# A spectral filter with a gated feed-forward block: the first product over two groups of 256 tokens, its weight tile loaded sooner and scaled alone, with four smaller edits

## The chip, the cores and the metric

The kernel runs on one core of a Trainium2 chip. The metric is device time in microseconds (us) of one execution. Before the change the median of three executions is 1207.04 us (1206.02 to 1208.09).

## The reference

One input `x` of 2048 tokens by 1024 features is normalised per token. The normalised rows `xn` go two ways: through a two-dimensional real FFT, a product with a complex filter and the inverse FFT (`s`), and through a feed-forward block with SiLU and 3584 hidden features. The output is the input plus the product of the two.

```
def _A_ref(x, w_r, w_i):
    X = rfft2(x, axes=(-2, -1))
    X = X * (w_r + 1j * w_i)
    return irfft2(X, (S, D), axes=(-2, -1))

def _B_ref(x, w1, w2):
    h = silu(einsum("bsd,df->bsf", x, w1))
    return einsum("bsf,fd->bsd", h, w2)

xn = layernorm(x)
s = _A_ref(xn, A_w_r, A_w_i)
g = silu(_B_ref(xn, B_w1, B_w2))
out = x + s * g
```

## The kernel before

Everything that TensorE multiplies is split into a high and a low float16 half, so each product is three matmuls: high by high, high by low, low by high. The tokens come in four chunks `c` of 512, each of four pieces `p` of 128 (a token of piece `p` of a chunk is every fourth row). The hidden features come in 28 tiles `f` of 128. The work has three long stages, and the spectral work is fed into the gaps between their matmuls.

**The first product** (`mm1`, matmuls on L500, PSUM tile `pa`) runs over pairs (c, f): 24 matmuls of 512 columns each, 8 slices of the 1024 features times 3 terms. The first six pairs are chunk 0 with f = 0 to 3, then chunk 1 with f = 0 and on. `evac` turns `pa` into hidden values with ScalarE. **The second product** (`mm2`, L584 to L586, PSUM tile `pb`) runs seven products `m` of eight blocks `j`, with weights `w2t` and hidden tiles `ht` read back from DRAM; `ht` has seven buffers, so a load of `ht` is issued when TensorE has done with an older one. The forward FFT along the features (`fa`), the filter stage (`fx`, L1070) and the inverse (`iu` on L1350 and L1358, `id` on L1439) are cut into small steps that a planner hands out between the matmuls.

The order of the instructions on every engine is fixed when the program is built, and each engine runs its own list in that order. Steps of the generators stand in lists: `bg` (layer norm, then the FFT stages) and `wq` (weights). At the start the order is written by hand in three tables: `FIRST` (the steps of the layer norm of chunk 0: `s` statistics, `n` normalise, `t` transpose on TensorE, `h` the high half, `l` the low half), `ENTRY` (what is done inside the first five products: `b` a step of `bg`, `w` a step of `wq`, `f` a group of 24 `fa` matmuls, `e` its evacuation) and `WARM` (idle matmuls on the constant `ones`, called `spin`, between steps).

What the change touches at the start:

- `weights1`: loads a raw tile `w1r` of w1, takes its largest absolute value with VectorE (`m`, L312), sums over partitions with a small TensorE matmul into the PSUM tile `s` (L293), makes a power of two from it (`e`, `r`, `rs` on L319 to L322, `s1` on GpSimd), then the high half `w` with ScalarE (L284) and the low half with VectorE (L287). Tiles 0 and 1 are scaled as a pair, 2 and 3 as a pair, 4 and 5 alone.
- `ln_gen`: statistics with VectorE (L780 to L783), the scale `v` with three small GpSimd operations (L785 to L787), the normalisation with ScalarE (L788). For chunk 0 TensorE transposes the pieces (PSUM tiles `tp`, L803 and L805); `hi` (L809) and `lo` (L816 with L817, or L819) write both halves of `xnT`. Pieces 0 to 2 transpose into the two large PSUM buffers `ft`, piece 3 into two small ones `ff`. Chunk 1 goes through `entering`: normalise into `xp` (L788), round to `xs` (L758), subtract for the low half (L766, VectorE), then four DMA transposes. On ScalarE's list the second pair of weight tiles (w_2, w_3) stands behind the normalisation of the first two pieces of chunk 1.
- The main body issues the loads on SP's queue: `x` pieces 0 to 3 and the identity, then `w1r` 0 to 2, then the constants.

What it touches later: `low_z` stores the filtered planes `zq` into `zd` (L1101 for even c, L1104 for odd c), `load_i` reads them back into `zt` with the constants `kk` (L1308 to L1312), `edge_in` copies one column into `zt` (L1319), `i_gen.mat` multiplies `zt` by `kk` (PSUM `iu`), `mat2` multiplies by the constants `ci` (PSUM `id`), and `edge_gen` has nine small float32 matmuls (`eps`, L1231 to L1233).

Of the kernel before, what the change touches and what calls it, by code (L numbers as in the profile page):

```python
# [25 lines left out]
WARM = [35, 8, 0, 0, 0, 12, 0, 0, 0, 0]  # L26
# [7 lines left out]
FIRST = ('s0 n0 s1 n1 t0 h0 s2 t1 h1 n2 s3 n3 l0', 't2 h2 t3 h3', 'l1 l2 l3')  # L34
ENTRY = ("fbwb||ew", "bbbwbb|bwwbb|f", "fwwbbw|wbbb|wb", "|wew|wf", "w||w")
# [118 lines left out]
def spectral_ffn(ctx, tc, x, w_r, w_i, w1, w2, ca, kc, ci, tw, pm, out):  # L154
    nc = tc.nc
# [21 lines left out]
    zd = [dp.tile([128, 2, 4, 2, 512] if c % 2 else [128, 4, 2, 1024], F16, name=f"zd{c}") for c in range(4)]  # L177
# [118 lines left out]
    def weights1():  # L296
# [43 lines left out]
        for i in range(3):  # L340
            load(i)
# [149 lines left out]
    def mm1(c, f, between={}):  # L491
        ps = J.pop("first", None) or pf.tile([128, 512], F32, name=f"pa{c}_{f}", tag="ff")
# [252 lines left out]
    def entering(c, stats, norm):  # L745
# [28 lines left out]
    def ln_gen(c):  # L774
# [17 lines left out]
        def trans(p):  # L792
            if p < 3:
                ps = pt.tile([128, 8, 128], F32, name=f"tp{c}_{p}", tag="ft")
                pst[p] = [(slice(0, 8), ps)]
            else:
                pst[p] = [(slice(d, d + 4), pf.tile([128, 4, 128], F32, name=f"tp{c}_{p}_{d}", tag="ff")) for d in (0, 4)]
            xt = A["x"].pop((c, p))
            xv = xt.rearrange("s (d0 d1) -> s d1 d0", d1=8)
            for ds, ps in pst[p]:  # L800
                for d in range(ds.start, ds.stop):
                    if p in (2, 3):
                        nc.tensor.matmul(ps[:, d - ds.start], xv[:, d], A["ident"], start=(d % 4 == 0), stop=(d % 4 == 3), is_transpose=True, skip_group_check=True)  # L803
                    else:
                        nc.tensor.transpose(ps[:, d - ds.start], xv[:, d], A["ident"])  # L805

        def hi(p):
            for ds, ps in pst[p]:
                nc.scalar.activation(xnT[c][:, 0, ds, p * 128:(p + 1) * 128], ps, AF.Copy)  # L809

        def lo(p):
            sl = slice(p * 128, (p + 1) * 128)
            for ds, ps in pst.pop(p):
                if p in (2, 3):
                    for d in range(0, ds.stop - ds.start, 4):
                        nc.tensor.matmul(ps[:, d:d + 4], A["minus"], xnT[c][:, 0, ds.start + d:ds.start + d + 4, sl], start=False, stop=True, skip_group_check=True)  # L816
                    nc.scalar.activation(xnT[c][:, 1, ds, sl], ps, AF.Copy)  # L817
                    continue
                nc.vector.tensor_tensor(xnT[c][:, 1, ds, sl], ps, xnT[c][:, 0, ds, sl], op=OP.subtract)  # L819
# [209 lines left out]
    def f_gen():  # L1029
# [174 lines left out]
    def edge_gen():  # L1204
# [96 lines left out]
    def load_i(c):  # L1301
        zt = C["p"].tile([128, 8192], F16, name=f"zt{c}", tag="zt", bufs=1)
        if c % 2:
            src = zd[c].rearrange("(m e) r q h x -> r m e (q h) x", e=2)
            dst = zt.rearrange("m (e k x) -> m e k x", e=2, k=8)
            for r in range(2):
                for e in range(2):
                    nc.sync.dma_start(dst[64 * r:64 * r + 64, e], src[r, :, e])  # L1308
# [259 lines left out]
    with tc.manual_schedule():  # L1568
# [73 lines left out]
        for k, q in enumerate((bg, wq, wq, bg, wq, wq, bg, wq, wq)):  # L1642
# [3 lines left out]
            if k == 4:  # L1646
                J["first"] = pf.tile([128, 512], F32, name="pa0_0", tag="ff")
# [150 lines left out]
```

## Time and profile before

| what | value |
|---|---|
| median of three executions | 1207.04 us |
| the profiled execution's own time | 1207.29 us |
| its span, first to last instruction | 1205.5 us |
| TensorE busy | 1195.1 us (99%) |
| VectorE busy | 1009.7 us (84%) |
| ScalarE busy | 511.6 us (42%) |
| GpSimd busy | 210.2 us (17%) |
| granted TensorE clock, mean | 0.999 of full speed |

Times are microseconds from the first instruction. PE is TensorE, DVE is VectorE, ACT is ScalarE, POOL is GpSimd, SP is the engine that issues nearly all DMAs. Matmuls are pipelined: each is shown some 0.16 us longer than the distance to the next one (a 512-column matmul is shown as 0.38 us and the next starts 0.216 us later), so work on TensorE is counted from start to start.

### The profile page before, as it was taken

The numbers are of one execution on the slowest core, as the hardware profiler recorded it, in microseconds if no ns is written. First come the engines' busy times: TensorE is split into PE (matmuls) and PEld (weight loads), VectorE is DVE, ScalarE is ACT, GpSimd is POOL, SyncE is SP. The second block draws the span as 40 slices with busy tenths as digits, with TensorE's granted clock in tenths as the row PEclk, the third lists the DMA queues.
The fourth block names the chain that finished last, engine by engine and source line by source line (L and its number), as shares of the span: only waits on it lengthen the run. The fifth ranks groups of instructions, "written<-read, shape, count | busy, mean of one in ns | idle before, by whom it ended". The sixth has DMA issues, their size and how long they took to land.

```text
span 1205.5 us, 18361 instructions
## 1 busy us (share of the span) xinstructions
PE 1195.1 (99%) x6600; PEld 597.1 (50%) x6600; DVE 1009.7 (84%) x1971; ACT 511.6 (42%) x698; POOL 210.2 (17%) x297
## 2 busy tenths in 40 slices
PE   8999999999999999999999999999999999999998
PEld 5544445444544544444444444445455545555555
DVE  7778986996799598669968999999279898998696
ACT  7775654366466463445524233132032222343212
POOL 2330041102402300411100111125031231100000
PEclk9999999999999999999999999999999999999999
DMA  8788698589989976889989999993997989989577
GB/s 263 182 192 213 199 268 242 173 248 281 294 251 278 275 227 197 195 197 205 183 234 246 284 239 261 237 305 131 261 333 219 367 308 329 363 319 343 175 242 267
DMA packets 279540, 302.24 MB, mean 251 GB/s; under 512 B 47956, under 2 KB 206932, under 8 KB 278548
## 3 DMA queue, kind: packets, MB, share of 16 engines
q1 hardware_dynamic: 275848, 291.69, 81.1%
q0 software_dynamic: 3312, 9.24, 4.5%
q8 instruction: 52, 0.85, 0.3%
q14 instruction: 40, 0.33, 0.1%
q10 hardware_dynamic: 288, 0.13, 0.0%
HBM read 183.94 MB, written 110.77 MB: 244 GB/s over the span
## 4 chain that ended last, share of the span: by engine, by line
PE 93%; DVE 3%; DMA 3%; issue 1%; SPq 1%; ACT 0%; POOL 0%; ACTq 0%; DVEq 0%
PE pa L500 48%; PE pb L584 12%; PE pb L585 12%; PE pb L586 12%; PE id L1439 2%; PE fx L1070 2%; DMA ht<-hd 2%; PE iu L1358 1%; PE iu L1350 1%; PE fa L837 1%; PE fa L838 1%; PE fa L839 1%; DMA w<-in_B_w_dram 0%; DVE Z L1192 0%; SPq L1104 0%
## 5 line engine op out<-in xcount | busy, mean ns | idle before, releaser
L500 PE MATMUL pa<-xnT,w 128*128 128x512 f16 x2688 | 584.0, 379 | 0.0
L500 PEld LDWEIGHTS <-w 128*128 128x128 f16 x2688 | 261.6, 98 | 311.9 <-issue 0.3
L584 PE MATMUL pb<-w,ht 128*128 128x512 f16 (+2 forms) x812 | 300.4, 372 | 1.0 <-DMA ht<-hd 1.0
L585 PE MATMUL pb<-w,ht 128*128 128x512 f16 (+2 forms) x812 | 300.4, 372 | 0.0
L586 PE MATMUL pb<-w,ht 128*128 128x512 f16 (+2 forms) x812 | 300.3, 372 | 0.0
L509 ACT ACTIVATE h<-pa,s 128x512 f32<-128x512 f32 x112 | 75.9, 681 | 153.4 <-PE pa L500 112.8
L586 PEld LDWEIGHTS <-ht 128*128 128x128 f16 x812 | 79.5, 98 | 91.0
L584 PEld LDWEIGHTS <-ht 128*128 128x128 f16 x812 | 79.5, 98 | 87.7 <-DMA ht<-hd 1.1
L585 PEld LDWEIGHTS <-ht 128*128 128x128 f16 x812 | 79.5, 98 | 86.5
L284 ACT ACTIVATE w<-jr,sc 128x512 f16<-128x512 f32 x98 | 67.5, 712 | 64.6 <-POOL jr L457 60.4
L287 DVE SCALAR_TENSOR_TENSOR hoone<-h,hs,hoone 128x2048 f16<-128x2048 f32 x28 | 65.6, 2342 | 17.0 <-ACT hoone L284 17.0
L287 DVE SCALAR_TENSOR_TENSOR w<-jr,sc,w 128x512 f16<-128x512 f32 x98 | 78.0, 803 | 0.0
L1192 POOL TENSOR_TENSOR Z<-yb 128x32 f32<-128x32 f32 x64 | 34.9, 573 | 224.9 <-DVE yb L1169 224.9
L284 ACT ACTIVATE hoone<-h,hs 128x2048 f16<-128x2048 f32 x28 | 55.9, 1997 | 18.4 <-DMA hd<-hoone 18.4
L457 POOL TENSOR_TENSOR jr<-jr,w 128x512 f32<-128x512 f32 x28 | 38.8, 1387 | 123.8 <-DMA w<-in_B_w_dram 75.9
L1092 ACT ACTIVATE zq<-Z,zs 128x1024 f16<-128x1024 f32 x16 | 18.4, 1148 | 91.5 <-DVE Z L1192 54.3
L287 DVE SCALAR_TENSOR_TENSOR hosum<-hr,hs,hosum 128x1536 f16<-128x1536 f32 x28 | 50.7, 1811 | 7.2 <-ACT hosum L284 7.2
L284 ACT ACTIVATE hosum<-hr,hs 128x1536 f16<-128x1536 f32 x28 | 43.9, 1569 | 20.5 <-DMA hd<-hosum 12.1
L539 DVE TENSOR_TENSOR hr<-h 128x1024 f32<-128x1024 f32 x28 | 34.1, 1218 | 18.3 <-ACT h L509 18.0
L678 ACT ACTIVATE pl<-pl,c 128x512 f32<-128x512 f32 (+2 forms) x28 | 17.4, 655 | 72.7 <-DVE pl L654 42.4
L284 ACT ACTIVATE w<-w1r,rs 128x1024 f16<-128x1024 f32 x28 | 32.0, 1143 | 27.8 <-DVE w L287 23.5
L1192 DVE TENSOR_TENSOR Z<-yb 128x128 f32<-128x128 f32 (+1 forms) x128 | 42.3, 398 | 0.0
(246 smaller groups left out, 1520.4 us busy)
## 6 DMA issues: line engine op xcount, KB each, us to landing
ht<-hd SPq DMA_DIRECT2D x112, 448.0 KB, 6.5
hd<-hoone SPq DMA_DIRECT2D x28, 1024.0 KB, 8.6
hd<-hosum SPq DMA_DIRECT2D x28, 768.0 KB, 5.5
w1r<-in_B_w_dram SPq DMA_DIRECT2D x28, 512.0 KB, 6.6
w2m<-in_B_w_dram SPq DMA_DIRECT2D x28, 512.0 KB, 6.4
jr<-in_B_w_dram SPq DMA_DIRECT2D x56, 256.0 KB, 6.2
ws<-wd SPq DMA_DIRECT2D x42, 256.0 KB, 4.4
jr<-ws SPq DMA_DIRECT2D x42, 256.0 KB, 6.2
```

The lines of the kernel that those rows point to most:

```text
L284: nc.scalar.activation(hi, raw, AF.Copy, scale=scale)
L287: nc.vector.scalar_tensor_tensor(lo, raw, scale, hi, op0=OP.mult, op1=OP.subtract)
L457: nc.gpsimd.tensor_tensor(raw[n], raw[n], more.pop(n), op=OP.add)
L500: nc.tensor.matmul(ps, w[:, wh, d], xt[:, xh, d], start=(n == 0), stop=(n == 23))
L509: nc.scalar.activation(hq[:, 2 * (c % 2) + f % 2], ps, AF.Silu, scale=s1[:, f:f + 1])
L539: tt(sums[:, 0:2], hq[:, 0::2], hq[:, 1::2], op=OP.subtract)
L584: nc.tensor.matmul(ps, hh[:, 0], w[:, 0], start=first, stop=False)
L585: nc.tensor.matmul(ps, hh[:, 0], w[:, 1], start=False, stop=False)
L586: nc.tensor.matmul(ps, hh[:, 1], w[:, 0], start=False, stop=last)
L1070: nc.tensor.matmul(o, k[:, c, kh], v[:, c, vh], start=(n == 0), stop=(n == 2))
L1192: eng.tensor_tensor(Z[:, ns, pos], x0[:, :, ls], x1[:, :, ls], op=o_)
L1439: nc.tensor.matmul(ps[:, g, cols], us[g][:, uh, 4 * r + p], C["ci"][:, ch, g, r, cols], start=(r == 0 and n == 0), stop=(r == 1 and n == 2 ...
```

## The change

- **First product in two halves.** Product (0, 0) runs over columns 0 to 255 (pieces 0 and 1), then over columns 256 to 511 (pieces 2 and 3): 48 matmuls of 256 columns in place of 24 of 512. Its steps between the matmuls may now be any number; `ENTRY[0]` and `FIRST` are rewritten for it. The 8 and 12 idle matmuls behind the transposes go; the 35 ahead of them stay.
- **Its w1 tile sooner and alone.** The load of `w1r` 0 is issued ahead of `x` pieces 2 and 3. Tile 0 is scaled by itself right behind the statistics of pieces 0 and 1, tile 1 by itself inside the first product. `w1t[0]` is set once the high half exists.
- **Transposes.** Piece 3 transposes into a large buffer `ft` too, in one tile.
- **One subtraction moves.** The low half of piece 0 of chunk 1 is made by GpSimd.
- **Four-plane rows.** For odd c, `zd` is laid out in groups of four planes of 64; stores go by half (512 rows of 256 elements), `load_i` loads `kk` first, then the first group of planes in four DMAs, and the second group two ticks later. The edge column lies in the first group.
- **Skipped zero columns.** In `mat2` the term with the low half of `ci` leaves out 127 columns that are zero where g = 0 and r = 1, and for g > 0 one column of r = 0 goes.
- **Merged edge matmuls.** Nine `eps` matmuls become three.

```diff
-WARM = [35, 8, 0, 0, 0, 12, 0, 0, 0, 0]
+WARM = [35, 0, 0, 0, 0, 0, 0]
-FIRST = ('s0 n0 s1 n1 t0 h0 s2 t1 h1 n2 s3 n3 l0', 't2 h2 t3 h3', 'l1 l2 l3')
-ENTRY = ("fbwb||ew", "bbbwbb|bwwbb|f", "fwwbbw|wbbb|wb", "|wew|wf", "w||w")
+TURNS = (2, 3)
+FIRST = ('s0 n0 s1 n1 t0 h0', 's2 t1 h1 n2 s3 n3 l0', 't2 h2 l1 t3 h3', 'l2 l3')
+ENTRY = ("bw|bw|ww|f|bwb|ew", "bbbwbb|bwwbb|f", "fwwbbw|wbbb|wb", "|wew|wf", "w||w")
-    zd = [dp.tile([128, 2, 4, 2, 512] if c % 2 else [128, 4, 2, 1024], F16, name=f"zd{c}") for c in range(4)]
+    zd = [dp.tile([128, 2, 2, 4, 2, 256] if c % 2 else [128, 4, 2, 1024], F16, name=f"zd{c}") for c in range(4)]
...
-        for i in range(3):
-            load(i)
+        load(0)
+        yield 0
+        load(1)
+        load(2)
...
-        for k in "m0 m1 p0 h0 l0 h1 l1 m2 m3 p2 h2 l2 h3 l3 m4 s4 h4 l4 m5 s5 h5 l5".split():
+        for k in "m0 s0 h0 l0 m1 s1 h1 l1 m2 m3 p2 h2 l2 h3 l3 m4 s4 h4 l4 m5 s5 h5 l5".split():
...
-        terms = [(d, wh, xh) for wh, xh in ((0, 0), (0, 1), (1, 0)) for d in range(8)]
+        terms = [(d, wh, xh, slice(0, 512)) for wh, xh in ((0, 0), (0, 1), (1, 0)) for d in range(8)]
         if f > 3 or c and f:
             terms.sort(key=lambda k: k[0])
-        for n, (d, wh, xh) in enumerate(terms):
+        if f == 0 and c == 0:
+            terms = [k[:3] + (slice(t, t + 256),) for t in (0, 256) for k in terms]
+        for n, (d, wh, xh, t) in enumerate(terms):
             if n in between:
                 between[n]()
-            nc.tensor.matmul(ps, w[:, wh, d], xt[:, xh, d], start=(n == 0), stop=(n == 23))
+            nc.tensor.matmul(ps[:, t], w[:, wh, d], xt[:, xh, d, t], start=(n % 24 == 0), stop=(n % 24 == 23))
...
-            nc.vector.tensor_tensor(split[:, p, 1], xn.pop(p), split[:, p, 0], op=OP.subtract)
+            (nc.gpsimd if p in (0,) else nc.vector).tensor_tensor(split[:, p, 1], xn.pop(p), split[:, p, 0], op=OP.subtract)
...
-                    for r in range(2):
-                        defer(1, lambda c=c, r=r: nc.sync.dma_start(zd[c][:, r, q], zv[:, :, c, 512 * r:512 * r + 512]))
+                    for h in range(2):
+                        defer(1, lambda c=c, h=h: nc.sync.dma_start(
+                            zd[c][:, :, :, q, h].rearrange("m r b x -> m (r b) x"), zv[:, h, c].rearrange("m (k x) -> m k x", k=4)))
...
-        for n in range(3):
-            nc.tensor.matmul(ps[:, n * 32 + 8:n * 32 + 32], perm[:, 0], rv[:, n, 1:4].rearrange("m q a r -> m (q a r)"), start=True, stop=True)
...
+        nc.tensor.matmul(p3[:, :, 8:32], perm[:, 0], r3[:, :, 8:32], start=True, stop=True)
+        nc.tensor.matmul(p3[:, :, 0:8], perm[:, 1], r3[:, :, 0:8], start=True, stop=False)
+        nc.tensor.matmul(p3[:, :, 0:8], perm[:, 2], r0.rearrange("m n a r -> m n (a r)"), start=False, stop=True)
...
         if c % 2:
+            nc.sync.dma_start(k, ki[c])
...
+            def part(b):
+                for r in range(2):
+                    for e in range(2):
+                        nc.sync.dma_start(dst[64 * r:64 * r + 64, e, b], src[r, :, e, b])
+
+            part(0)
+            defer(2, lambda: part(1))
...
-                for r, cols in enumerate((slice(0, 130), slice(0 if g == 0 else 127, 256))):
+                for r, span in enumerate((slice(0, 129 if g else 130), slice(127 if g else 0, 256))):
                     for n, (uh, ch) in passes:
+                        cols = slice(127, 256) if r and ch else span
...
+        w1j = add(wq, weights1())
+        slot(wq)
         for i in range(2, 4):
             load_x(0, i)
...
-        for k, q in enumerate((bg, wq, wq, bg, wq, wq, bg, wq, wq)):
+        for k, q in enumerate((bg, wq, wq, wq, bg)):
...
-                ev = mm1(c, f, {8: enter[0], 16: enter[1]})
+                ev = mm1(c, f, {8 * k + 8: step for k, step in enumerate(enter[:-1])})
```

Two stretches of VectorE's list show what that does to the order at the start. In the names, `st` and `mv` are the statistics of a piece of tokens (st_2 is piece 2), `w1r` a raw weight tile, `m` its maxima, `s_0` the small sum from TensorE, `e`, `r` and `rs` the scales. The first stretch begins behind the statistics of piece 1. Before:

```order
L783 BN_AGGR mv_1_317<-st_1_314 128x2
L780 BN_STATS st_2_334<-x_2_249 128x6
L781 BN_STATS st_2_334<-x_2_249 128x6
L783 BN_AGGR mv_2_337<-st_2_334 128x2
L780 BN_STATS st_3_354<-x_3_251 128x6
L781 BN_STATS st_3_354<-x_3_251 128x6
L783 BN_AGGR mv_3_357<-st_3_354 128x2
L819 TENSOR_TENSOR xnT_303<-tp_0_324,xnT_303 128x8x128
L312 TENSOR_REDUCE m_219<-w1r_254 128x1
L312 TENSOR_REDUCE m_219<-w1r_256 128x1
L319 TENSOR_SCALAR e_218<-s_0_402 128x2
```

In the same place of VectorE's list now:

```order
L790 BN_AGGR mv_1_317<-st_1_314 128x2
L313 TENSOR_REDUCE m_219<-w1r_249 128x1
L320 TENSOR_SCALAR e_218<-s_0_339 128x1
L321 TENSOR_SCALAR e_218<-e_218 128x1
L322 RECIPROCAL r_220<-e_218 128x1
L323 TENSOR_SCALAR rs_221<-r_220 128x1
L787 BN_STATS st_2_348<-x_2_251 128x6
L788 BN_STATS st_2_348<-x_2_251 128x6
L790 BN_AGGR mv_2_351<-st_2_348 128x2
L787 BN_STATS st_3_368<-x_3_253 128x6
L788 BN_STATS st_3_368<-x_3_253 128x6
L790 BN_AGGR mv_3_371<-st_3_368 128x2
```

The maximum of the first weight tile and the whole of its scale now stand ahead of the statistics of pieces 2 and 3.

Further down VectorE's list, at the low half of the first weight tile (`w_0`), the statistics of piece 0 of chunk 1 (`st_0`) followed at once before:

```order
L819 TENSOR_TENSOR xnT_303<-tp_1_343,xnT_303 128x8x128
L287 SCALAR_TENSOR_TENSOR w_0_425<-w1r_254,rs_221,w_0_425 128x1024
L780 BN_STATS st_0_479<-x_0_301 128x6
L781 BN_STATS st_0_479<-x_0_301 128x6
L783 BN_AGGR mv_0_482<-st_0_479 128x2
```

Now the second weight tile stands between them, with `e` waiting for the sum `s_1`:

```order
L288 SCALAR_TENSOR_TENSOR w_0_346<-w1r_249,rs_221,w_0_346 128x1024
L313 TENSOR_REDUCE m_219<-w1r_256 128x1
L320 TENSOR_SCALAR e_218<-s_1_437 128x1
L321 TENSOR_SCALAR e_218<-e_218 128x1
L322 RECIPROCAL r_220<-e_218 128x1
L323 TENSOR_SCALAR rs_221<-r_220 128x1
L327 TENSOR_TENSOR ep<-e_218 128x1
L328 TENSOR_TENSOR hs<-r_220 128x1
L787 BN_STATS st_0_494<-x_0_301 128x6
```

On TensorE's list `s_1` stands behind half of the first product's first 24 matmuls and the transposes: transposes of piece 0, `s_0`, transposes of piece 1, 8 matmuls of 256 columns, transposes of pieces 2 and 3, 8 matmuls, 4 matmuls with `minus` (the low halves of pieces 2 and 3), 8 matmuls, `s_1`, 8 matmuls, 24 `fa` matmuls, 16 matmuls, then product (0, 1).

SP's list at the first load of `zt`, before (`ht` are hidden tiles, `jr` and `w_3` weights of the second product):

```order
L560 DMA ht_0_1_8085<-hd_0_90 128x1792
L560 DMA ht_1_0_8087<-hd_0_90 128x1792
L1308 DMA zt_8117<-zd_86 64x4096 x4
L1312 DMA kk_8122<-in_kc_dram 128x2064
L447 DMA jr_8127<-in_B_w_dram 128x512
L452 DMA w_3_0_7523<-in_B_w_dram 128x512
L560 DMA ht_1_1_8155<-hd_0_90 128x1792
L560 DMA ht_2_0_8157<-hd_0_90 128x1792
```

And SP's list there now:

```order
L567 DMA ht_0_1_8086<-hd_0_90 128x1792
L567 DMA ht_1_0_8088<-hd_0_90 128x1792
L1308 DMA kk_8119<-in_kc_dram 128x2064
L1315 DMA zt_8118<-zd_86 64x2048 x4
L452 DMA jr_8128<-in_B_w_dram 128x512
L457 DMA w_3_0_7530<-in_B_w_dram 128x512
L567 DMA ht_1_1_8156<-hd_0_90 128x1792
L567 DMA ht_2_0_8158<-hd_0_90 128x1792
L1315 DMA zt_8118<-zd_86 64x2048 x4
```

`kk` has moved ahead of `zt`, and half of `zt` behind the two hidden tiles.

## Rows read from the trace of the kernel before

**Rows 1.** The page: busy time of each engine, share of the span, instructions.

```profile
PE 1195.1 (99%) x6600; PEld 597.1 (50%) x6600; DVE 1009.7 (84%) x1971; ACT 511.6 (42%) x698; POOL 210.2 (17%) x297
```

**Rows 2.** Timeline of TensorE at the start: start, duration, instruction, idle before.

```profile
0.99 6.47 PE L1622 MATMUL spin<-ones 128*128 128x256 f16 x35 [0.99 <-POOL ones L1614]
8.90 1.15 PE L805 MATMUL tp<-ident,x 128*128 128x128 f32 x8 [1.44 <-ACT x L788]
...
11.24 1.04 PE L1622 MATMUL spin<-ones 128*128 128x256 f16 x8
13.64 2.28 PE L803 MATMUL tp<-ident,x 128*128 128x128 f32 x16 [1.37 <-ACT x L788]
...
21.16 7.07 PE L500 MATMUL pa<-xnT,w 128*128 128x512 f16 x32
...
31.27 1.89 PE L500 MATMUL pa<-xnT,w 128*128 128x512 f16 x8
```

**Rows 3.** Timeline of TensorE around the first `iu` matmuls.

```profile
875.33 0.38 PE L586 MATMUL pb<-w,ht 128*128 128x512 f16 x1
876.26 1.50 PE L1350 MATMUL iu<-kk,zt 128*128 128x128 f16 x24 [0.55 <-DMA kk<-in_kc_dram]
878.71 0.39 PE L584 MATMUL pb<-w,ht 128*128 128x512 f16 x1 [0.96 <-DMA ht<-hd]
```

**Rows 4.** Timelines of SP and VectorE ahead of these.

```profile
858.11 2.94 SPq L1308 DMA_DIRECT2D zt<-zd  x4
...
865.55 2.58 SPq L560 DMA_DIRECT2D ht<-hd  x2
...
875.51 0.21 DVE L1319 COPY zt<-zps 128x16 f16<-128x16 f16 x1 [12.02 <-DMA jr<-in_B_w_dram]
```

**Rows 5.** Timeline of TensorE around the edge matmuls.

```profile
814.70 0.30 PE L1231 MATMUL eps<-edge,perm 128*128 128x24 f32 x2
...
816.62 0.38 PE L584 MATMUL pb<-w,ht 128*128 128x512 f16 x1
```

**Rows 6.** Chain of waits: start, time from start to start, what.

```profile
798.64 1.31 PE fx L1070 x12
...
926.86 1.53 PE id L1439 x24
```

**Rows 7.** Timeline of VectorE at the start.

```profile
8.70 0.69 DVE L780 BATCH_NORM_STATS2 st<-x 128x6 f32<-128x512 f32 x1 [1.07 <-DMA x<-in_A_x_dram]
...
11.41 0.21 DVE L783 BATCH_NORM_AGGREGATE mv<-st 128x2 f32<-128x12 f32 x1
...
19.26 0.69 DVE L780 BATCH_NORM_STATS2 st<-x 128x6 f32<-128x512 f32 x1
...
34.82 1.21 DVE L312 TENSOR_REDUCE m<-w1r 128x1 f32<-128x1024 f32 x1
36.51 0.16 DVE L319 TENSOR_SCALAR e<-s 128x1 int32<-128x1 int32 x1 [0.48 <-PE s L293]
...
37.09 0.15 DVE L322 TENSOR_SCALAR rs<-r 128x1 f32<-128x1 f32 x1
```

**Rows 8.** Timeline of ScalarE at the start.

```profile
7.61 2.58 ACT L788 ACTIVATE x<-x,v 128x1024 f32<-128x1024 f32 x2 [0.83 <-POOL v L787]
...
23.11 2.18 ACT L788 ACTIVATE xp<-x,v 128x1024 f32<-128x1024 f32 x1 [0.67 <-POOL v L787]
...
28.50 1.06 ACT L758 ACTIVATE xs<-xp 128x1024 f16<-128x1024 f32 x1
29.82 1.15 ACT L284 ACTIVATE w<-w1r,rs 128x1024 f16<-128x1024 f32 x1 [0.27 <-DVE rs L322]
```

**Rows 9.** Timeline of GpSimd: the scale of two pieces of chunk 1.

```profile
21.30 1.42 POOL L786 TENSOR_TENSOR v<-v,mhalf 128x1 f32<-128x1 f32 x1
...
24.22 0.55 POOL L786 TENSOR_TENSOR v<-v,mhalf 128x1 f32<-128x1 f32 x1
```

**Rows 10.** DMA issues between 6 and 8 us: size, us from issue to landing.

```profile
w1r<-in_B_w_dram SPq DMA_DIRECT2D x1, 512.0 KB, 10.5
```

**Rows 11.** Timeline of SP at the start: pieces 2 and 3 of `x` go out.

```profile
2.13 0.91 SPq L710 DMA_DIRECT2D x<-in_A_x_dram  x2
```

More of the change, by code (lines that the diff above doesn't have):

```diff
@@ L334, in split @@
             high(new[i][:, 0], raw[i], rs[:, i:i + 1])
+            if i == 0:
+                w1t[0] = new[0]
         def rest(i):
@@ L491, in mm1 @@
     def mm1(c, f, between={}):
[L492 removed]
+        ps = pf.tile([128, 512], F32, name=f"pa{c}_{f}", tag="ff")
         w, xt = w1t[f], xnT[c]
[L494 removed]
+        terms = [(d, wh, xh, slice(0, 512)) for wh, xh in ((0, 0), (0, 1), (1, 0)) for d in range(8)]
         if f > 3 or c and f:
             terms.sort(key=lambda k: k[0])
[L497 removed]
+        if f == 0 and c == 0:
+            terms = [k[:3] + (slice(t, t + 256),) for t in (0, 256) for k in terms]
+        for n, (d, wh, xh, t) in enumerate(terms):
             if n in between:
                 between[n]()
[L500 removed]
+            nc.tensor.matmul(ps[:, t], w[:, wh, d], xt[:, xh, d, t], start=(n % 24 == 0), stop=(n % 24 == 23))
         if c == 3:
@@ L792, in trans @@
         def trans(p):
[L793 to L797, printed above, removed]
+            ps = pst[p] = pt.tile([128, 8, 128], F32, name=f"tp{c}_{p}", tag="ft")
             xt = A["x"].pop((c, p))
             xv = xt.rearrange("s (d0 d1) -> s d1 d0", d1=8)
[L800 to L805, printed above, removed]
+            for d in range(8):
+                if p in TURNS:
+                    nc.tensor.matmul(ps[:, d], xv[:, d], A["ident"], start=(d % 4 == 0), stop=(d % 4 == 3), is_transpose=True, skip_group_check=True)
+                else:
+                    nc.tensor.transpose(ps[:, d], xv[:, d], A["ident"])
@@ L807, in hi @@
         def hi(p):
-            for ds, ps in pst[p]:
-                nc.scalar.activation(xnT[c][:, 0, ds, p * 128:(p + 1) * 128], ps, AF.Copy)
+            nc.scalar.activation(xnT[c][:, 0, :, p * 128:(p + 1) * 128], pst[p], AF.Copy)
         def lo(p):
             sl = slice(p * 128, (p + 1) * 128)
[L813 to L819, printed above, removed]
+            ps = pst.pop(p)
@@ L821, in ln_gen @@
+            if p not in TURNS:
+                nc.vector.tensor_tensor(xnT[c][:, 1, :, sl], ps, xnT[c][:, 0, :, sl], op=OP.subtract)
+                return
+            for d in (0, 4):
+                nc.tensor.matmul(ps[:, d:d + 4], A["minus"], xnT[c][:, 0, d:d + 4, sl], start=False, stop=True, skip_group_check=True)
+            nc.scalar.activation(xnT[c][:, 1, :, sl], ps, AF.Copy)
         new_xnT(c)
@@ L1229, in edge_gen @@
         ps = pf.tile([128, 512], F32, name="eps", tag="ff")
-        for n in range(3):
-            nc.tensor.matmul(ps[:, n * 32 + 8:n * 32 + 32], perm[:, 0], rv[:, n, 1:4].rearrange("m q a r -> m (q a r)"), start=True, stop=True)
-            nc.tensor.matmul(ps[:, n * 32:n * 32 + 8], perm[:, 1], rv[:, n, 0].rearrange("m a r -> m (a r)"), start=True, stop=False)
-            nc.tensor.matmul(ps[:, n * 32:n * 32 + 8], perm[:, 2], r0[:, n].rearrange("m a r -> m (a r)"), start=False, stop=True)
+        p3 = ps[:, 0:96].rearrange("m (n x) -> m n x", n=3)
+        r3 = rv.rearrange("m n q a r -> m n (q a r)")
+        nc.tensor.matmul(p3[:, :, 8:32], perm[:, 0], r3[:, :, 8:32], start=True, stop=True)
+        nc.tensor.matmul(p3[:, :, 0:8], perm[:, 1], r3[:, :, 0:8], start=True, stop=False)
+        nc.tensor.matmul(p3[:, :, 0:8], perm[:, 2], r0.rearrange("m n a r -> m n (a r)"), start=False, stop=True)
         yield 1
@@ L1302, in load_i @@
         zt = C["p"].tile([128, 8192], F16, name=f"zt{c}", tag="zt", bufs=1)
+        k = C["p"].tile([128, 2064], F16, name=f"kk{c}", tag="kk", bufs=1)
         if c % 2:
[L1304 to L1308, printed above, removed]
+            nc.sync.dma_start(k, ki[c])
+            src = zd[c].rearrange("(m e) r b q h x -> r m e b (q h x)", e=2)
+            dst = zt.rearrange("m (e b x) -> m e b x", e=2, b=2)
+            def part(b):
[4 more added lines that the diff above has]
+            defer(2, lambda: part(1))
         else:
             nc.sync.dma_start(zt.rearrange("m (q h x) -> m q h x", q=4, h=2), zd[c])
-        k = C["p"].tile([128, 2064], F16, name=f"kk{c}", tag="kk", bufs=1)
-        nc.sync.dma_start(k, ki[c])
+            nc.sync.dma_start(k, ki[c])
         C["z"][c], C["k"][c] = zt, k
@@ L1619, in spin @@
             if n:
-                ps = pf.tile([128, 512], F32, name="spin", tag="ff") if "first" not in J else J["first"]
+                ps = pf.tile([128, 512], F32, name="spin", tag="ff")
                 for _ in range(n):
@@ L1645, in spectral_ffn @@
                 load_x(1, 1)
-            if k == 4:
-                J["first"] = pf.tile([128, 512], F32, name="pa0_0", tag="ff")
             spin(WARM[1 + k])
```

11 lines of the change are left out of this document (5 added, 6 removed).

## Prediction

> **What bounds the kernel now.** I read the page's busy line first [rows 1]: TensorE is busy 99% of the span and the others are far from it, so an edit pays only if it takes instructions off TensorE or ends a time in which it has nothing to do. Then I read TensorE's timeline for such times. At the start it waits several times before 13.64, and from the 16 transposes there it runs back to back [rows 2]. The one later place that any edit touches is near 876, where it waits 0.55 us for `kk` and 0.96 us for `ht` [rows 3]. Then I took distances from start to start. A 512-column matmul costs (7.07 − 0.38)/31 = 0.216 us in the run of 32 `pa` [rows 2], a 256-column one 1.31/12 = 0.109 [rows 6], a 128-column one about (1.50 − 0.2)/23 = 0.057 [rows 3]. Last I followed the chain on ScalarE, VectorE and GpSimd that leads to product (0, 2), because its weight comes just in time.
>
> The sum goes against the profiled execution's 1207.29 us; the median is 0.25 below that, and I take the 0.25 off at the end.
>
> **The change part by part: what goes.**
>
> *The wait at 876.* `iu` starts at 876.26 and could have started at 875.33 + 0.216 = 875.55, so 0.71 us is lost. Behind its 24 matmuls (1.34 us) `pb` could start at 877.60 and starts at 878.71, so another 1.11 is lost [rows 3]; together 1.82. Four `zt` transfers of 2.1 MB in all are issued from 858.11, ahead of the two `ht` of 865.55 [rows 4], and the `ht` land only as `pb` starts. Half of `zt` (1.05 MB) now goes behind the `ht`. At the page's mean of 251 GB/s that is 4 us less ahead of them, against the 1.11 us needed. `kk`, which ended the first wait, goes ahead of everything. The copy of the edge column at 875.51 [rows 4] needs only the first half of `zt`. The second half of `zt` is next to be late; its consumers stand behind further `pb` products, so I cost it at nothing. −1.82 us; bounds 0 and −1.82.
>
> *The edge matmuls.* Nine take from 814.70 to 816.62 [rows 5], 0.21 each. Three stay: −6 × 0.21 = −1.25. Joined ones have three times the columns; if columns alone cost, a part comes back. Bounds −1.0 and −1.3.
>
> *The zero columns.* For each of 16 tiles one `id` matmul falls from 256 to 129 columns, and a few lose one column: 0.109 − 0.057 = 0.052 each, with the single columns 0.057. 24 `id` take 1.53 us now [rows 6], so TensorE, with nothing idle between, bounds them. −0.91 us; bounds −0.8 and −0.95.
>
> *The four-plane stores and loads.* Packets of 512 bytes in place of 1 KB for odd `c`. No matmul waits for the stores. A wait of SP's queue of about a microsecond would reach loads that have several microseconds of room. 0; bounds 0 and +1.
>
> Steady part: −1.82 − 1.25 − 0.91 = −3.98 us.
>
> **The start.** The 20 idle matmuls that go stood in waits: the 8 from 11.24 end before 12.3, and the next transposes begin at 13.64 behind ScalarE [rows 2]. They gain nothing. The 256-column halves cost the same columns as before (48 × 0.109 against 24 × 0.216, +0.05), and 24 of them (2.6 us) can now run in those gaps. But the transposes of pieces 2 and 3 themselves move:
>
> 1. The first `w1r` takes the place of `x` piece 2 in SP's queue, which goes out at 2.13 [rows 11] and had landed at 8.70 [rows 7]. It has the same 512 KB in shorter pieces; I take 9.0. A reduce of 1.21 ends at 10.2; the small sum and `e` follow 0.48 later, as with the third weight group; `rs` ends 0.73 behind `e` (36.51 to 37.24) [rows 7], at 11.4.
> 2. On VectorE's list the statistics of piece 2 now stand behind `rs`. They start at 11.4 instead of 8.70, 2.7 later. From them to the last aggregate's end it is 11.62 − 8.70 = 2.92 [rows 7], so 14.3. Scale and normalisation of piece 3 follow as before: the transpose of piece 3 starts near 17.0 and ends near 18.1, against 15.9 [rows 2].
> 3. Behind it stand 8 half matmuls (0.87), 4 with `minus` (0.86), 8 more (0.87), then `s_1`, at 20.7. `e` of tile 1 is at about 21.1, and the statistics of piece 0 of chunk 1 stand behind that scale: 21.9 in place of 19.26 [rows 7], +2.65.
> 4. From these statistics to ScalarE's normalisation into `xp` was 23.11 − 19.26 = 3.85 [rows 7, 8]; so 25.75. On ScalarE's list two normalisations with their roundings stand ahead of w_2: 2 × (2.18 + 1.06), 6.45 with small gaps, as from 23.11 to 29.56 [rows 8]; so 32.2. The high half of w_2 takes 1.15 [rows 8]: 33.35. Before it ended at 30.97 and product (0, 2) began at 31.27 [rows 2], so 0.3 us of room was there.
> 5. TensorE itself reaches product (0, 2) at about 31.6: product (0, 1) starts at 21.16 + 16 × 0.216 = 24.62 before [rows 2], and near 24.95 now, because the transposes end 2.2 later while 24 half matmuls were pulled ahead and the idle ones went. From there 6.65 as before. So a new stall of 1.75 stands ahead of (0, 2), which begins at 33.4, 2.1 later than 31.27. TensorE has work without a gap behind that, so nothing absorbs it.
>
> Bounds of this: step 4's 3.85 contains a GpSimd operation of 1.42 us, which took 0.55 in the next piece [rows 9]; the slow one lay beside a VectorE operation with two tensor inputs. If the order now keeps them apart it is 0.87 less, and if the tile lands earlier another 0.35 (then the transposes limit): +0.9. On the other side, a `w1r` issued between 6 and 8 us took 10.5 us to land [rows 10]; from 2.13, where piece 2 of `x` went out [rows 11], that would be 12.6. That load stood behind three others, so I take the middle of 8.70 and 12.6 as the late bound, 10.6, some 1.5 behind my 9.0: +3.6. I take +2.1, because behind the aggregate of piece 0 a two-input operation (the low half of w_1) still stands on VectorE. The Trainium skill ("GPSIMD Engine Reference", section 1, Specifications) says that GpSimd shares its SBUF interfaces with VectorE and that instructions with two SBUF inputs contend; the two rows agree, and by that rule the sum stays at +2.1 and does not fall to +0.9.
>
> *The subtraction on GpSimd* frees VectorE of some 1.2 us and the chain above does not contain it; 0, because ScalarE ends that chain. *The load of `w1r` 0 by itself* costs no more bytes.
>
> **Sum:** 1207.29 − 3.98 + 2.1 = 1205.4 on the profiled basis, **1205.2** on the median's.
>
> **The rivals.**
>
> *The start costs little* (0 to +0.9). For it: the fast GpSimd row [rows 9], and a tile that lands early. Against it: five steps on one chain, each in list order. 1207.04 − 3.98 + 0.9 = 1204.0, down to 1202.9 if nothing is lost at all.
>
> *The clock falls*, and the change ends slower than before. From 7.46, when the 35 idle matmuls end, to about 15.5 TensorE would have only transposes and 8 half matmuls, without the 8 idle ones in between. The first 35 took 6.47 us where 35 × 0.109 = 3.82 is the full level: 2.65 us of low level (1.2 GHz, not 2.4) before it rose [rows 2, 6]. Paid once more it is 1207.04 − 3.98 + 2.1 + 2.65 = 1207.8; paid twice, because TensorE's work there is broken by waits, 1210.5. It decides against the change from 1.9 us on. Against it: before, after 3.8 us with 16 transposes alone (7.46 to 11.24), the 8 idle matmuls took 1.04 us, which is the full level [rows 2]. The Trainium skill ("TensorE: Matmul & The Clock Gate", Part 4, PE-mode transpose) says that transposes do not count as busy in the way matmuls do; the row does not show that for 3.8 us, and no row shows it for 8.
>
> *The wait at 876 stays*, because the queue and not its order delays `ht`: +1.82, 1207.0. The stretch ahead of it is one of the fullest of DMA, but the bytes ahead of `ht` do fall.
>
> *The first tile lands late*: +3.6 in place of +2.1, with more behind it, about 1206.7 to 1208.8.
>
> **How the numbers follow.** Forecast 1205.2: 0.38. Start cheap, 1204.0: 0.34. Clock falls: 0.16. Wait stays: 0.06. Late tile: 0.06. Two tenths of a per cent is 2.4 us here, about what a measurement of this kernel can tell from no change; so faster is below 1204.6 and slower above 1209.5. Faster takes the cheap start and a small part of the forecast's own spread: 0.36. Slower takes the upper half of the clock's case and the end of the late tile's: 0.10. Same 0.54. The range 1202.9 to 1208.4 holds the first two cases, the wait that stays and the lower part of the clock's case.
>
> **What would show it.** Right: statistics of piece 2 near 11.4 and of chunk 1's piece 0 near 21.9 on VectorE; product (0, 2) starting near 33.4 with a wait for ScalarE's `w`; no wait on TensorE at the first `iu`; edge matmuls in about 0.7 us; 24 `id` in about 1.45. Cheap start: product (0, 2) before 32.3. Clock: half matmuls 0.2 apart instead of 0.109. It would be wrong if TensorE met a new wait where the second half of `zt` or the longer list of stores is late, or if the freed GpSimd and ScalarE work moved something I have not followed.

## The result and the profile after

The changed kernel takes 1212.78 us (median of 6, 1211.03 to 1214.86) where the kernel before takes 1206.89 (median of 6). The ratio is 1.0047 (95% interval 1.0037 to 1.0058): 5.9 us slower, and above the whole range that I gave. The profiled execution took 1213.61 us and spans 1211.8.

The page shows first that TensorE is no longer the only bound. It is busy 2.3 us less than before [rows 1], although the span is 6.3 us longer, so about 8.6 us of new waits must lie on it. Then the chain that ended last, by engine; before it was `PE 93%; DVE 3%; DMA 3%`:

```profile
PE 1192.8 (98%) x6594; PEld 596.5 (49%) x6594; DVE 1011.7 (83%) x1974; ACT 512.9 (42%) x696; POOL 213.4 (18%) x299
...
PE 64%; DVE 17%; DMA 13%; issue 3%; SPq 2%; ACT 1%; POOL 0%; DVEq 0%; ACTq 0%; POOLq 0%
```

A third of the time now leads through VectorE, SP's queue and DMAs. The waits of TensorE, with what ended them, the sum in us, the count and the longest:

```profile
PE tp L807 <- ACT x L795: 2.0, 1, 2.0
PE pa L507 <- ACT xnT L810: 1.9, 1, 1.9
PE id L1449 <- DVE us L1438: 1.9, 2, 1.5
PE iu L1359 <- DMA jr<-in_B_w_dram: 1.9, 1, 1.9
PE iu L1359 <- DVE ub L1376: 1.8, 1, 1.8
PE pa L507 <- ACT w L285: 1.4, 1, 1.4
...
PE iu L1367 <- DVE ub L1376: 0.5, 1, 0.5
PE iu L1367 <- POOL zt L1331: 0.2, 1, 0.2
```

The two waits near 876 [rows 3] are gone. In their place stand six waits in the inverse stage (`iu`, `id`), which before had none behind 879, and one on the weight w_2 (`pa <- ACT w`).

The second tool is the offset: the start of the same block of TensorE's list after, less before. TensorE's order is the same from the third product on, so each step of the offset is one cause.

| at (us of before) | place | offset | step |
|---|---|---|---|
| 43 | behind the first products | +3.05 | the start |
| 817 | behind the edge matmuls | +1.72 | −1.33 |
| 876 | first `iu` | +1.00 | −0.72 |
| 879 | the `pb` behind it | −0.11 | −1.11 |
| 889, 895 | third and fourth `iu` | +1.89, +3.86 | +3.97 |
| 922 | first `id` done | +5.30 | +1.44 |
| 922 to 1045 | next chunks | +6.76 | +1.46 |
| 1155 | end | +6.35 | columns |

So in this execution every saving that I forecast came, to a tenth. The six late waits add some 7.2 us (6.25 in the rows before rounding, plus 0.16 each that the shown ends of matmuls hide), and the skipped columns take off 0.84 over 16 tiles. The sum: 1207.29 + 3.05 − 1.33 − 1.83 − 0.84 + 7.2 = 1213.5, against 1213.61.

Where the late waits come from shows on the other engines. First SP, ahead of the first `iu`, start and duration of each issue:

```profile
872.01 4.12 SPq L1315 DMA_DIRECT2D zt<-zd  x4
876.23 0.53 SPq L452 DMA_DIRECT2D jr<-in_B_w_dram  x1
876.86 0.38 SPq L457 DMA_DIRECT2D w<-in_B_w_dram  x1
```

The second half of `zt` occupies the queue for 4.1 us, and the `w` that was issued at 872.77 before goes out behind it, at 876.86. GpSimd, ScalarE and VectorE follow in one line:

```profile
887.05 1.27 POOL L462 TENSOR_TENSOR jr<-jr,w 128x512 f32<-128x512 f32 x1 [8.84 <-DMA w<-in_B_w_dram]
...
888.35 0.72 ACT L285 ACTIVATE w<-jr,sc 128x512 f16<-128x512 f32 x1 [8.91 <-POOL jr L462]
888.98 0.58 ACT L1373 ACTIVATE uc<-iu 128x512 f32<-128x512 f32 x1
...
889.59 0.69 DVE L1375 TENSOR_TENSOR ub<-iu,uc 128x512 f32<-128x512 f32 x1 [8.76 <-ACT uc L1373]
890.19 0.68 DVE L1376 TENSOR_TENSOR ub<-iu,uc 128x512 f32<-128x512 f32 x1
```

`uc` copies the result of the first `iu`, which TensorE began at 877.26 and had finished at 878.8. It waits ten more microseconds for nothing of its own: ahead of it on ScalarE's list stands the high half of a weight of the second product, which waits for that `w`. The same three steps before:

```profile
872.77 0.33 SPq L452 DMA_DIRECT2D w<-in_B_w_dram  x1
...
881.38 1.34 POOL L457 TENSOR_TENSOR jr<-jr,w 128x512 f32<-128x512 f32 x1 [2.41 <-DMA w<-in_B_w_dram]
...
883.38 0.58 ACT L1364 ACTIVATE uc<-iu 128x512 f32<-128x512 f32 x1
```

So the `w` goes out 4.1 us later and then takes 1.6 us longer until GpSimd has it (10.2 in place of 8.6); `uc` is 5.6 later. VectorE's whole inverse stage starts with it, and TensorE's third `iu` needs the PSUM buffer that the second `ub` empties at 890.87; it starts at 891.02. The row above names a DMA of `jr` as its releaser; the `ub` is the one that ended then.

### The profile page after: what moved, and what is told of

It is laid out like the page before. It is cut to its first block, busy times and chain, and to the rows that moved or that the text cites. A ratio compares the mean times of both kernels' runs of the same rounds, so it can differ in the third digit from the quotient of the medians.

```text
span 1211.8 us, 18363 instructions
## 1 busy us (share of the span) xinstructions
PE 1192.8 (98%) x6594; PEld 596.5 (49%) x6594; DVE 1011.7 (83%) x1974; ACT 512.9 (42%) x696; POOL 213.4 (18%) x299
## 4 chain that ended last, share of the span: by engine, by line
PE 64%; DVE 17%; DMA 13%; issue 3%; SPq 2%; ACT 1%; POOL 0%; DVEq 0%; ACTq 0%; POOLq 0%
PE pa L507 47%; PE pb L591 4%; PE pb L592 4%; PE pb L593 4%; DMA jr<-ws 3%; DMA ht<-hd 2%; DVE Z L1194 2%; DVE w L288 2%; DMA vr<-rd 1%; PE id L1449 1%; DMA jr<-in_B_w_dram 1%; DMA kk<-in_kc_dram 1%; DMA fs<-sd 1%; DVE uu L1408 1%; DVE zq L1098 1%
## 5 line engine op out<-in xcount | busy, mean ns | idle before, releaser
L507 PE MATMUL pa<-xnT,w 128*128 128x512 f16 (+1 forms) x2712 | 584.5, 377 | 3.3 <-ACT xnT L810 1.9
L285 ACT ACTIVATE hosum<-hr,hs 128x1536 f16<-128x1536 f32 x28 | 43.9, 1569 | 15.4 <-DMA hd<-hosum 11.5
```

The lines of the kernel that those rows point to most:

```text
L285: nc.scalar.activation(hi, raw, AF.Copy, scale=scale)
L507: nc.tensor.matmul(ps[:, t], w[:, wh, d], xt[:, xh, d, t], start=(n % 24 == 0), stop=(n % 24 == 23))
```

## Experiments

The ratio is always to the kernel before on the same chip. Each diff shows the heart of the edit.

**The parts by themselves.** a1 has the edits of the start alone, a2 the four-plane rows alone, a3 the edge matmuls and columns, a4 all but the start (a2 and a3).

```diff
# a1
+FIRST = ('s0 n0 s1 n1 t0 h0', 's2 t1 h1 n2 s3 n3 l0', 't2 h2 l1 t3 h3', 'l2 l3')
+ENTRY = ("bw|bw|ww|f|bwb|ew", ...
# a2
+            nc.sync.dma_start(k, ki[c])
+            part(0)
+            defer(2, lambda: part(1))
# a3
+        nc.tensor.matmul(p3[:, :, 8:32], perm[:, 0], r3[:, :, 8:32], start=True, stop=True)
+                        cols = slice(127, 256) if r and ch else span
```

a1: 

> Only the edits of the start (first product in two halves, its tile sooner and alone, transposes, one subtraction on GpSimd); rows of zd and zt, zero columns and edge matmuls as before. Theory A (VectorE runs without a gap from 640 to 848, and its list, not TensorE's, sets when the inverse stage starts; the start delays both by 3.05): the whole 3.05 and some 1 to 2 more, 1210 to 1212. Theory B (the second half of zt and its shorter rows on SP's queue cost the 6.5 us behind 884): 3.05 and no more, 1209.9, with the waits at 876 as before.

a2: 

> Only the four-plane rows: zd's layout, its stores by half, kk first, zt in two parts. Theory A: the waits of 0.55 and 0.96 us at 876 go, and come back between 884 and 925 because VectorE is no sooner: 1206.9 within 1. Theory B: the waits at 876 go (-1.8) and 6.5 us of waits on ub, us and jr appear: 1211.5.

a3: 

> Only the merged edge matmuls and the skipped zero columns. By my prediction's terms -1.33 and -0.84: 1204.7. Theory A: the 1.33 is waited away at 876, since zt comes when VectorE and SP let it; only the columns stay, some 1206.1.

a4: 

> All but the start. By my prediction's terms 1206.9 - 3.98 = 1202.9. Theory A: waits between 884 and 925 eat all but the columns: about 1206. Theory B: 1206.9 + 6.5 - 3.98 = 1209.4.

| run | median us | ratio, 95% interval |
|---|---|---|
| a1 | 1210.76 | 1.0041 (1.0027 to 1.0055) |
| a2 | 1209.73 | 1.0034 (1.0021 to 1.0047) |
| a3 | 1206.81 | 1.0004 (0.9987 to 1.0021) |
| a4 | 1210.49 | 1.0031 (1.0017 to 1.0044) |

a1 loses 4.9 us. In its profile TensorE is 3.4 late at 817 and 4.4 at the first `iu`, because its wait for `kk` has grown from 0.55 to 1.6: the one microsecond more that theory A gave.

The rows, which I had costed as a gain of 1.82, lose 4 us without any other edit. In a2 the waits at 876 are gone, and one of the inverse stage is there:

```profile
PE iu L1357 <- DVE ub L1374: 2.9, 1, 2.9
```

In a2 VectorE copies the edge column at 871.32, 4.2 us sooner than before [rows 4], so `zt` did come sooner, and yet `uc` is at 884.75, 1.4 later. That is theory B's mark and speaks against theory A, by which VectorE would be the late one. Theory A has its part elsewhere: in a3's trace the edge matmuls bring 1.41 us at 817, and 0.86 of it is waited away at 876, where `kk` now keeps `iu` for 1.4 us. The interval of a3 runs from −1.6 to +2.5 us: it leaves out the −2.2 that my terms add up to, and can't tell theory A's −0.8 from nothing.

**VectorE's list.** b3 is the kernel before with less work on VectorE.

```diff
-            tt(Y[:, :, 0], t1[:, :, 0], t2[:, :, 1], op=OP.subtract)
-            tt(Y[:, :, 1], t1[:, :, 1], t2[:, :, 0], op=OP.add)
```

> The kernel before without two operations of VectorE in each of the 16 filter steps (the subtraction and the addition that join the two products with the filter): 32 x 0.6 us less on VectorE between 535 and 848, with the same order on all engines. Its output is not the reference's. If VectorE's list sets when zt and ht come: zt's issue moves from 858 to earlier, both waits at 876 go, 1206.2 - 1.5 = 1204.7 or less. If SP or the DMA queues set it: both waits stay, 1206.2.

1205.17 us, ratio 0.9986 (0.9977 to 0.9995). `zt` goes out at 851.28 instead of 858.11 [rows 4], and TensorE has no wait left behind the start; these are all that the view has:

```profile
PE tp L805 <- ACT x L788: 2.4, 2, 2.2
PE tp L803 <- ACT x L788: 1.4, 1, 1.4
PE spin L1622 <- POOL ones L1614: 1.0, 1, 1.0
```

So the waits at 876 are set by VectorE: from 640 to 848 it is idle for 4 us of 208, its last step there is `zp`, and SP's list stands still until `zp` is stored:

```profile
842.75 0.26 DVE L1279 SCALAR_TENSOR_TENSOR zp<-edge,zs,zp 128x32 f16<-128x32 f32 x1 [1.50 <-ACT zp L1278]
```

(this is before; after it is at 847.68). Theory A holds for 876. A gain of TensorE ahead of it, as that of the edge matmuls, is only worth something if the loads behind `zp` are shortened too.

**The order on SP's queue.** b1 is a4 with the second half three steps later, b2 is a4 with both halves at once, c1 is the changed kernel with b1's edit.

```diff
# b1, c1
-            defer(2, lambda: part(1))
+            defer(5, lambda: part(1))
# b2
-            defer(2, lambda: part(1))
+            part(1)
```

b1: 

> As a4 (all but the start), with the second half of zt issued three steps later, behind two more hidden tiles and the weights that ScalarE waits for. Theory B as it stands after a2 (the four transfers of the second half hold SP's queue for 4.6 us; the weights w behind them come later, ScalarE waits for these ahead of uc, VectorE starts the inverse stage late): uc near 881 to 883 instead of 886.5, the waits of TensorE on ub and us gone, 1202.5 to 1204. Theory A (VectorE's list to 848 sets it): uc and the time stay, 1210.

b2: 

> As a4, with both halves of zt issued at once behind kk, as the four transfers of before were; the short rows stay. If the order on the queue is what costs: the wait for ht at 876 is back (about 1 us) and uc comes as early as before, 1205 to 1206. If the shorter rows cost by themselves: uc stays late, 1209 to 1211.

c1: 

> The changed kernel, and nothing else than the second half of zt three steps later. If its place on SP's queue made all of the 6.5 us of waits behind 884, as b1 against a4 says: 1212.8 - 6 = 1206.8, and what is left against b1 is the start, +2.5 to +3.4. If VectorE's own lag (4.9 us at 848 where TensorE's is 1.7) makes part of them: 1208 to 1210, with waits on ub and us left.

| run | median us | ratio, 95% interval | `uc` behind the first `iu` |
|---|---|---|---|
| before | | | 7.1 us |
| a4 | 1210.49 | 1.0031 (1.0017 to 1.0044) | 12.4 |
| b1 | 1204.32 | 0.9976 (0.9968 to 0.9985) | 4.9 |
| b2 | 1207.94 | 1.0012 (0.9999 to 1.0024) | 9.6 |
| the changed kernel | 1212.78 | 1.0047 (1.0037 to 1.0058) | 11.7 |
| c1 | 1207.04 | 0.9994 (0.9981 to 1.0007) | 5.6 |

This settles what made the change slower. One number, the place of four DMA issues, is worth 0.55% between a4 and b1 and 0.53% between the changed kernel and c1, some 6.5 us both times. SP and ScalarE in b1:

```profile
868.53 0.33 SPq L452 DMA_DIRECT2D w<-in_B_w_dram  x1
...
874.38 3.01 SPq L1314 DMA_DIRECT2D zt<-zd  x4
...
878.42 0.72 ACT L284 ACTIVATE w<-jr,sc 128x512 f16<-128x512 f32 x1 [2.54 <-POOL jr L457]
879.05 0.58 ACT L1372 ACTIVATE uc<-iu 128x512 f32<-128x512 f32 x1
```

and the one wait of TensorE that is left behind its start:

```profile
PE iu L1358 <- DMA zt<-zd: 0.4, 1, 0.4
```

The `w` that ScalarE waits for goes out 5.9 us ahead of the second half and `uc` is 4.3 us sooner than before; the halved `zt` is itself only 0.4 late. From the issue of this `w` to GpSimd's sum that reads it, it is 10.2 to 10.6 us where the half was issued just ahead of it (the changed kernel, a4, a2) and 7.3 to 8.6 where it was not (before, b1, c1). In a2 the `w` even goes out 0.6 sooner than before, at 872.19, and is there 1.5 later. The Trainium skill ("DMA: Bandwidth & Descriptors", section "Queues, rings and completion order") says that each DMA engine consumes the descriptors of a ring in their order; that a `w` issued behind the half comes late and one issued ahead of it does not agrees with this. b1 gains 2.9 us where I had forecast 3.98 for all but the start. c1 also rules out that VectorE's lag made the late waits: there `zp` is at 846.28, 3.5 us later than before, with TensorE only 0.2 later at 817, and the waits on `ub` and `us` are gone all the same.

b2 shows the other end. With both halves ahead of `ht` the wait that the edit was meant to remove is longer than ever:

```profile
PE pb L584 <- DMA ht<-hd: 3.5, 1, 3.5
```

On SP's queue, the last six of the eight transfers of `zt`:

```profile
860.01 7.56 SPq L1314 DMA_DIRECT2D zt<-zd  x6
```

The eight issues hold the queue from 858.85 to 867.57, 8.7 us, where the four of before took 2.94 for the same bytes [rows 4]. Whether it is the number of transfers or the 512-byte pieces that were stored just ahead of them, I haven't separated. `uc` is where it was before (883.80 against 883.38), and the time lies between the two that I expected.

c4 has a3's edits and moves `kk` ahead of `zt`, with the rows of before.

```diff
+            nc.sync.dma_start(k, ki[c])   # ahead of zt
```

> As a3 (merged edge matmuls, skipped columns, rows as before), with kk ahead of zt and nothing else moved. If b1's gain needs the halved zt: the wait for ht stays 1 us, that for kk turns into one for zt, 1206. If kk alone was late: 1205.2.

1208.22 us, 0.9996 (0.9979 to 1.0013): no gain to be seen. Its profiled execution was one of the longer ones (span 1211.2; `zp` at 846.11, TensorE 1.4 us later from 780 on), and `iu` waited 6.4 us in it, so its trace can't be set against the others. It doesn't show whether halving is needed.

**The clock behind the late waits.** In six of these profiles the granted clock falls to the lower level (1.2 GHz) beside a long wait of TensorE in this stage: for 3.4 us in a2, a4, b4 and c3, for 6.8 us in b2 and c4. In the changed kernel's own profile it does not fall there. a2 by window (length; busy time of PE, PEld, DVE, ACT, POOL; then the granted clock, DMA share, GB/s), first the wait, then the stretch behind it:

```profile
893.00:896.00 3.00, 0.07 (x1) 0.00 (x0) 3.00 (x7) 1.67 (x2) 0.15 (x1) 1.00 0.90 292
896.10:899.50 3.40, 3.40 (x27) 2.84 (x28) 3.37 (x10) 0.57 (x1) 1.55 (x1) 0.50 1.03 399
```

From the fourth `iu` to the first `id` it is 25.7 us in a2 and 24.0 before, with no wait between, so 1.7 of a2's loss is the clock's. Read in the same way from start to start, less the waits, it is 1.5 in a4 and 2.7 in b2. The late waits thus cost more than their own length in these runs, b2's time is its wait for `ht` and the clock, and some 1.5 us of what lies between the profiles of a4 and b1 is the clock. The 7.2 us of the changed kernel's profile are waits alone.

**The start.** b4 is the changed kernel with the statistics of piece 0 of chunk 1 ahead of the scale of tile 1, c2 is b4 with c1's edit, c3 is the changed kernel with 23 idle matmuls in TensorE's waits at 11.5 and 14.5.

```diff
# b4, c2
-ENTRY = ("bw|bw|ww|f|bwb|ew", ...
+ENTRY = ("bw|bbw|ww|f|wb|ew", ...
# c3
-WARM = [35, 0, 0, 0, 0, 0, 0]
+WARM = [35, 0, 0, 0, 0, 16, 0]
+            if c == 0 and p == 2:
+                A["spin"](7)
```

b4: 

> The changed kernel with the statistics of piece 0 of chunk 1 ahead of the scale of tile 1 on VectorE. If it is the place of these statistics that delays w_2: they start near 17.8 instead of 22.6, the normalisation near 25.2 instead of 26.4 (it still stands behind the evacuation of fa on ScalarE), and product (0, 2) near 32.7 instead of 33.95. If TensorE's slow transposes set it: no move.

c2: 

> The changed kernel with the second half of zt later and the statistics of piece 0 of chunk 1 ahead of the scale of tile 1. By b1 (1204.3) and the start of b4 (+0.5): 1204.8. If the start of b4 was fast only because the clock did not fall in it: some 1206.

c3: 

> The changed kernel with 16 idle matmuls behind the transposes of piece 1 and 7 ahead of those of piece 2, in TensorE's waits. If the emptier stretch lets the clock fall: granted clock 1.0 between 15.6 and 19 (it was 0.50 and 0.64), the 16 transposes in 2.3 instead of 3.4 us, s_1 some 0.7 sooner, product (0, 2) at 33.2. If the clock fell for another reason: 0.5 again.

TensorE in the changed kernel, start, duration and idle before:

```profile
13.72 1.03 PE L507 MATMUL pa<-xnT,w 128*128 128x256 f16 x8 [1.95 <-ACT xnT L810]
15.63 3.40 PE L805 MATMUL tp<-ident,x 128*128 128x128 f32 x16 [0.89 <-ACT x L795]
...
21.48 0.28 PE L294 MATMUL s<-m,ones 128*128 128x1 f32 x2
...
33.95 1.90 PE L507 MATMUL pa<-xnT,w 128*128 128x512 f16 x8 [1.38 <-ACT w L285]
```

and two stretches of it by window (columns as above):

```profile
15.60:17.60 2.00, 1.97 (x9) 1.97 (x10) 2.00 (x2) 1.24 (x1) 0.08 (x1) 0.50 0.99 377
17.60:19.00 1.40, 1.40 (x11) 1.38 (x10) 1.34 (x2) 1.02 (x1) 0.00 (x0) 0.64 1.05 333
```

The clock did fall, to the lower level (1.2 GHz), and the 16 transposes took 3.40 us; before they took 2.28 [rows 2] at full clock. In c3, with idle matmuls in the waits, the same stretches stand at 1.00:

```profile
14.51 0.93 PE L1634 MATMUL spin<-ones 128*128 128x256 f16 x7
15.56 1.14 PE L807 MATMUL tp<-ident,x 128*128 128x128 f32 x8
16.94 1.16 PE L807 MATMUL tp<-ident,x 128*128 128x128 f32 x8 [0.23 <-ACT x L795]
...
20.55 0.28 PE L294 MATMUL s<-m,ones 128*128 128x1 f32 x2
```

`s_1` is 0.93 sooner and the offset behind the first products is +2.13 instead of +3.05. The time, 1213.2 (1.0052, 1.0030 to 1.0075), is too coarse for 0.9 us. The clock is not low there in every execution: a1 and c1 show it, b4 and c2, with the same matmuls on TensorE up to there and waits of about the same length, do not. The Trainium skill ("TensorE: Matmul & The Clock Gate", Part 4, PE-mode transpose) says that transposes do not count as busy as matmuls do; that the clock fell where the idle matmuls were taken out, and stood where they were put back, agrees with it, but the executions without them in which it stood show that it is no certainty.

b4 and c2 tell the rest. c2 and c1 differ only in the place of the statistics, and the first tile landed alike in both (`e` of tile 0 at 10.02, where the profile above has 10.84). Product (0, 2) in c1, then in c2:

```profile
32.41 1.90 PE L507 MATMUL pa<-xnT,w 128*128 128x512 f16 x8 [1.39 <-ACT w L285]
```

```profile
30.87 1.90 PE L507 MATMUL pa<-xnT,w 128*128 128x512 f16 x8 [0.15 <-ACT w L285]
```

1.54 us sooner, and 0.4 sooner than before [rows 2]. The clock has little part in it: in c1 it was low under the first eight half matmuls (1.86 us in place of 1.03), the wait behind them took that up, and `s_1` starts at 19.93 against 19.80 in c2. The offset behind the first products is +1.49 in c1 and −0.05 in c2, in b4 +0.49. So the start's cost is a load with which `e` comes 0.8 us earlier or later, a clock that may fall (0.1 in c1, 0.9 in the changed kernel) and the place of one statistics step (1.5). b4's one time is 1214.8: it keeps the late waits (`uc` at 890.01), and its profile has a wait of 2.2 us for `ht` at 878 besides. c2 takes 1206.39, 0.9996 (0.9977 to 1.0015): no longer slower, but nothing shown beyond b1, which stays the best: the old start, and the rest of the change with the second half of `zt` later.

## Why the prediction was wrong

**The step that failed is the one on the four-plane rows.** I looked at who consumes the second half of `zt` and found it far away: "its consumers stand behind further `pb` products, so I cost it at nothing". That was true, and beside the point. What came late was what stands behind it on SP's queue: a weight tile (issued at 876.86 in place of 872.77, and 1.6 us longer on its way), then ScalarE's list behind that weight, then `uc`, then VectorE's inverse stage. I had also written that a wait of SP's queue "would reach loads that have several microseconds of room", with an upper bound of 1 us, without looking which load on the queue has the least room. The row was there: before, `uc` at 883.38 was already 5.6 us behind the end of its `iu`, kept by the same weight. I had named the second half as what could make the forecast wrong, but as data that TensorE waits for. It measured +7.2 us in place of 0.

**The wait at 876:** −1.82 forecast, −1.83 measured (0.72 and 1.11). The halving and the earlier `kk` did what the bytes ahead of `ht` said, in a2 and a4 as well; in b4's one profile, though, a wait for `ht` (2.2) is there again. b3 adds what I didn't see: VectorE's list is what made these loads late.

**The edge matmuls:** −1.25 forecast, −1.33 measured. The joined matmuls have more columns and cost no more (three in 0.59 us, 0.20 each, against 0.21), so here the price lay in their number.

**The columns:** −0.91 forecast, −0.84 measured.

**The start:** +2.1 forecast, +3.05 measured, inside the bounds. The chain went as put: statistics of piece 2 at 11.49 (11.4 forecast), of chunk 1 at 22.59 (21.9), w_2 ready at 33.9 (33.35), product (0, 2) at 33.95 (33.4) with a wait for `w`. The cheap start did not come: on the way to the normalisation GpSimd again had one slow operation (1.04 us at 24.34, where the same one took 0.19 for the next piece). What the chain is later than put is the clock's work: c3 prices the slow transposes at 0.9, so without them the chain would have come 0.35 sooner than I had it. The clock was my rival with a chance of 0.16 and a price of 2.65 or more (2.5 without the shown end of the last matmul); at the start it came in part of the executions and cost a third of that or less. That it could also fall behind late waits, as in a2, a4 and b2, I had not thought of. The last 0.35 lie at tile 4, whose maximum VectorE now has too late: TensorE's next small sum waits 0.23 for `m`. That wait was in none of my steps.

**The subtraction on GpSimd** was costed at nothing, and no run tries it alone; it takes 2.14 us there (29.79 to 31.93) and GpSimd's next scale starts only behind it, at 32.01. ScalarE uses that scale at 35.41 and does not wait for it.

The chances were wrong as the sum was: 0.10 for slower came from the clock and a late tile, none from a queue that the change makes longer in the middle.

## What to carry to other kernels

When a transfer is moved on a queue, cost it for what stands behind its new place and not only for its consumer: find on each list the instruction with the least room, follow it across lists to the end, and move the transfer behind that one. Here the same halved load loses or gains with its place (1.0031 and 0.9976). A gain on the engine that is busy 99% is only safe up to the next place where another engine's list has as little room: a view by list, with the offsets of both kernels side by side, shows it where the busy shares don't.

## What the chip showed that I had not expected

The DMA engines are as busy while `zt` is read as at other times, but move half as much. Before, in two windows of 6 us (columns as above):

```profile
862.00:868.00 6.00, 6.00 (x30) 2.70 (x29) 1.35 (x2) 0.00 (x0) 0.00 (x0) 1.00 1.03 198
874.00:880.00 6.00, 4.49 (x38) 2.61 (x37) 0.83 (x2) 1.00 (x2) 1.26 (x1) 1.00 1.03 377
```

198 GB/s against 377 at the same share. The slow stretch goes with the transfers: with `zt` issued at 851.28 (b3) it is 856 to 868 (217 and 214 GB/s). Costing a moved transfer by its bytes at the mean rate can therefore be wrong by about two; why `zt` moves so slowly, I haven't tried.

VectorE's `zp` came between 841.4 and 848.6 in the thirteen profiled executions in which VectorE had its full work. The new start makes part of that, but c4 with the old one had it at 846.1 where the six others with the old one lie between 841.4 and 843.1. As VectorE is idle for only 4 of the 208 us from 640 to 848, what it loses once (at the store of a hidden tile near 638, or near 734) stays. Part of the 3 to 10 us between executions of one kernel may be that, and part the clock behind late waits; I haven't shown it.
